# Moving a token block's second layer from float32r to float16 in a three-block attention and feed-forward kernel

## The chip, the cores and the metric

The kernel runs on one core of a Trainium2 chip. The metric is the time of the whole program on the device, in microseconds (us), as the median of several runs. A separate execution is recorded by the hardware profiler; everything said of engines comes from that one.

## The reference, cut to what matters

```
scores = scale * q @ k^T                      # 4 batches, 8 heads, 576 queries, 64 dims
thresh = max(scores) - tau                    # per query
scores = where(scores >= thresh, scores, -1e9)
x = softmax(scores) @ v                       # then heads side by side: x is 2304 x 512
xn = x / sqrt(mean(x*x) + 1e-6) * rms_g       # layer 1 only
y = (silu(xn @ w_gate) * (xn @ w_val)) @ w_out      # 512 -> 1536 -> 512
out = (silu(y @ w_gate2) * (y @ w_val2)) @ w_out2   # layer 2, without the norm
```

All inputs and outputs are float32.

## The kernel before, in words

The 2304 tokens are three blocks `b` of 768 (`TW`), each kept transposed as four chunks of 128 features. A block goes through attention, then the rms norm and layer 1 (`m` = 0), then layer 2 (`m` = 1). A layer is 18 units (`NU`): twelve gate/value units (`gate_val`) of 128 hidden features, with two out units (`outp`) behind every four of them; an out unit makes two of the four output chunks. Unit `n` counts through all blocks and layers, 36 per block: block 1's layer 1 is 36 to 53, its layer 2 is 54 to 71, block 2 has 72 to 89 and 90 to 107. The attention of block `b`+1 is laid between the units of block `b`; block 2's attention lies between units 36 and 53, in block 1's layer 1.

A float32 product is made of operands split into a high and a low part: high·high, high·low and low·high. An ordinary gate/value unit is 48 matmuls of 128 x 384 (`dense`, L1075). A seven-product unit (`gate_val7`, chosen by `fewer`) takes the fast 2 x 2 scheme with seven products of six matmuls (L1112), 42 in all. It needs four combinations of the input's quarters (`combine`: differences on VectorE L930, high parts on ScalarE L931, low parts L934) and, for each unit, sums of the weights' quarters (`weights7`: a load from the kept copy `kept`, four sums L1042, casts L1045, low parts L1047). Before, unit 54 is ordinary, 55 to 71 are seven-product units in float32r, and the gate/value units of 72 to 107 (`H16`) are seven-product units in float16.

Float16 needs scales, powers of two made from sums of squares. `square_sum` (L863, L864) loads a kept weight and squares it on ScalarE; `h_square` (L893) squares the hidden values of layer 1; `spread_sums` (L878) adds the partitions with a matmul; `power` (L869 to L872) makes the power of two in four VectorE steps; `unit_scales` (L887, L888) makes the factors of each unit. `y_scale` (L897 to L903) does this for layer 2's input and scales the layer-1 output `Y` on ScalarE; the last addition to `Y` (L1258) takes the same scale. The weights are scaled on ScalarE (L1040) ahead of their sums. Before, `square_sum` runs for block 2's layer-1 weights in block 1's layer 2, and for its layer-2 weights and out weights in block 2's layer 1.

`rms` makes the norm: the sums of squares of x (tile `SS`) by matmuls (L818), a reciprocal root in VectorE steps (L827 to L837), a spread over the partitions by matmuls (L849), and four multiplications (L858). `put` writes the high and low part of a layer's input (L952, L955). `split_h` makes high and low part of the hidden values (L1212, L1216).

What sets the order: every instruction is handed to `Program.op` with an engine, a cost, what it reads and writes, and a due time `p`, mostly the planned start of its unit `SU(n)` plus an offset of a table (`OFFS`, `GP`). `Program.order` runs a list scheduler over them, and each engine then does its instructions in that fixed order. All large transfers are issued by one queue, SP. While block 2's attention runs, gate and out products have two PSUM banks (`pt0`, `pt1`); four more (`pbPD`, `pbPA`, `pbPB`) come as the attention stages end.

## Time and profile before

| | us |
|---|---|
| median of 3 runs | 1145.5 (1144.47 to 1147.23) |
| profiled execution | 1140.48 |
| its span, first to last instruction | 1138.7 |
| units 36 to 53 (block 1, layer 1; attention of block 2) | 499 to 721 |
| units 54 to 71 (block 1, layer 2) | 721 to 868 |
| units 72 to 89 (block 2, layer 1) | 868 to 1003 |
| units 90 to 107 (block 2, layer 2) | 1003 to 1139 |

Busy time is the time in which an engine executes; for TensorE's matmuls, which overlap, the spacing from start to start is the price of one. The chain of waits goes back from the last instruction to what released it. A list of waits gives, for an engine, the line that waited, what ended the wait, and the total, the number and the longest in us.

### The profile page before, as it was taken

What the parts mean: (1) busy time and instruction counts of PE and PEld (TensorE: products, weight loads), DVE (VectorE), ACT (ScalarE), POOL (GpSimd) and SP (SyncE); (2) the same over time, 40 slices, a digit from 0 to 9 for tenths busy, and PEclk for the clock granted to TensorE, in tenths of its full rate; (3) what the DMA queues carried; (4) which work ended last, traced back from release to release, by engine and by line L of the source; (5) the groups of instructions that cost most, each with busy time, mean ns of one, the idle gap of its engine ahead of it and who ended that gap; (6) DMA issues with size and microseconds to landing.
All of it is one profiled execution on the core that took longest, in us unless ns stands there. A gap on an engine that the chain in (4) does not pass through costs nothing.

```text
span 1138.7 us, 19685 instructions
## 1 busy us (share of the span) xinstructions
PE 1106.7 (97%) x7106; PEld 965.3 (85%) x7106; DVE 906.8 (80%) x1631; ACT 791.4 (69%) x1175; POOL 630.6 (55%) x831
## 2 busy tenths in 40 slices
PE   8989999999999999999999999999999999999998
PEld 5656889989999989999999998999997768668677
DVE  7899498888987888887888887886688757985954
ACT  5798689878889887745866555756685766766631
POOL 5576145765668887449799875143413253234711
PEclk8999899999999999999999999999999999999999
DMA  6564349999999989958788786733755232122111
GB/s 186 172 221 143 103 126 288 266 268 305 236 243 261 237 266 262 262 177 198 165 188 184 182 187 147 260 110 128 255 191 178 74 115 98 60 108 93 37 39 56
DMA packets 178898, 201.44 MB, mean 177 GB/s; under 512 B 144368, under 2 KB 148208, under 8 KB 168816
## 3 DMA queue, kind: packets, MB, share of 16 engines
q1 hardware_dynamic: 178512, 200.18, 62.3%
q8 instruction: 56, 0.92, 0.3%
q14 instruction: 42, 0.34, 0.1%
q10 hardware_dynamic: 288, 0.00, 0.0%
HBM read 135.66 MB, written 36.18 MB: 151 GB/s over the span
## 4 chain that ended last, share of the span: by engine, by line
PE 60%; DVE 12%; DMA 10%; ACT 7%; POOL 6%; issue 4%; SPq 0%; ACTq 0%; POOLq 0%; DVEq 0%
PE ps L1075 20%; PE pbPA L1112 7%; PE pt L1112 7%; PE pbPB L1075 5%; DMA w<-kept 5%; PE pbPD L1075 5%; DMA arena<-arena 3%; PE pt L1075 3%; PE ps L719 2%; PE pt L772 2%; PE pt L675 2%; PE ps L615 2%; POOL arena L578 1%; PE pt L654 1%; ACT w L864 1%
## 5 line engine op out<-in xcount | busy, mean ns | idle before, releaser
L1075 PE MATMUL ps<-XS,w 128*128 128x384 f32 x1152 | 211.2, 340 | 2.6 <-DVE th L1194 1.4
L1075 PEld LDWEIGHTS ps<-XS,w 128*128 128x128 f32 x1152 | 200.6, 190 | 4.1 <-DVE th L1194 1.7
L1112 PEld LDWEIGHTS <-arena 128*128 128x128 f16 x1008 | 97.3, 98 | 65.7 <-issue 2.9
L1216 POOL TENSOR_TENSOR h<-th,h 128x384 fp32r<-128x384 f32 (+1 forms) x39 | 62.6, 1616 | 119.7 <-ACT h L1212 119.5
L1075 PE MATMUL pt<-XS,w 128*128 128x384 f32 x600 | 110.8, 337 | 2.8 <-DVE th L1178 2.8
L1075 PE MATMUL ps<-h,w 128*128 128x384 f32 x576 | 105.7, 338 | 2.6 <-DVE col L734 1.3
L1075 PEld LDWEIGHTS pt<-XS,w 128*128 128x128 f32 x600 | 103.0, 188 | 4.9 <-DVE th L1178 4.4
L1075 PEld LDWEIGHTS ps<-h,w 128*128 128x128 f32 x576 | 99.7, 188 | 4.9 <-issue 2.0
L735 ACT ACTIVATE arena<-ps,col 128x576 f32<-128x576 f32 x96 | 70.4, 736 | 39.4 <-DVE col L734 22.3
L733 DVE TENSOR_REDUCE col<-ps 128x1 f32<-128x576 f32 x96 | 71.4, 751 | 25.7 <-PE ps L719 25.6
L736 DVE SCALAR_TENSOR_TENSOR arena<-ps,col,arena 128x576 f32<-128x576 f32 x96 | 77.5, 810 | 14.5 <-ACT arena L735 13.9
L1075 PE MATMUL pbPB<-h,w 128*128 128x384 f32 x420 | 81.6, 340 | 1.9 <-DVE h L1216 1.8
L1212 ACT CAST h<-th 128x768 fp32r<-128x768 f32 x72 | 59.8, 832 | 33.9 <-DVE th L1175 13.2
L1112 PE MATMUL pt<-rx,arena 128*128 128x384 f16 (+1 forms) x384 | 82.9, 329 | 0.0
L1075 PE MATMUL pbPD<-h,w 128*128 128x384 f32 x420 | 79.9, 339 | 1.3 <-DVE h L1216 1.3
L578 POOL TENSOR_TENSOR arena<-arena 128x512 f16<-128x512 f32 x68 | 81.0, 1193 | 0.1
L1047 POOL TENSOR_TENSOR arena<-w,arena 128x384 f16<-128x384 f32 (+3 forms) x48 | 59.0, 1254 | 39.3 <-ACT arena L1045 39.1
L1112 PE MATMUL pbPA<-rx,arena 128*128 128x384 f16 (+1 forms) x368 | 78.7, 330 | 1.4 <-DVE X L858 0.9
L559 ACT ACTIVATE arena<-arena,col 128x576 f32<-128x576 f32 x76 | 65.0, 865 | 17.0 <-DVE col L746 9.3
L1075 PEld LDWEIGHTS pbPB<-h,w 128*128 128x128 f32 x420 | 73.4, 188 | 3.5 <-DVE h L1216 2.5
L1075 PEld LDWEIGHTS pbPD<-h,w 128*128 128x128 f32 x420 | 73.4, 188 | 2.2 <-DVE h L1216 1.7
L742 POOL TENSOR_SCALAR col<-col 128x1 f32<-128x1 f32 x96 | 32.7, 341 | 74.3 <-DVE arena L736 56.1
(274 smaller groups left out, 2733.5 us busy)
## 6 DMA issues: line engine op xcount, KB each, us to landing
w<-kept SPq DMA_DIRECT2D x77, 512.0 KB, 4.1
w<-in_w SPq DMA_DIRECT2D x36, 1024.0 KB, 7.0
w<-kept SPq DMA_DIRECT2D x25, 1024.0 KB, 5.7
kept<-w SPq DMA_DIRECT2D x17, 1024.0 KB, 5.3
kept<-w SPq DMA_DIRECT2D x26, 512.0 KB, 4.3
arena<-in_qkv SPq DMA_DIRECT2D x40, 160.0 KB, 4.3
ra<-in_qkv SPq DMA_DIRECT2D x10, 576.0 KB, 4.6
out<-Y SPq DMA_DIRECT2D x11, 384.0 KB, 2.7
```

Of the source, the lines that this page charges most:

```text
L559: op("ACT", 760, lambda: nc.scalar.activation(e, e, AF.Identity, bias=c[:, 4:5], scale=c[:, 3:4]), **k)
L578: op(en, 601 if eng == 2 else 1128, lambda: n1.tensor_tensor(h[:, 640:], e[:, :512], h[:, :512], ALU.subtract), lock=True, w=[("lo", n)], ...
L615: nc.tensor.matmul(s[m:m + w, jj, :b - a], x[k, c0:c0 + w], x[k, S + a:S + b], start=True, stop=True)
L733: op("DVE", 670, lambda: nc.vector.tensor_reduce(c[:, 0:1], s2, AX.XY, ALU.max, negate=True), w=[*sk, ("mx", n)], bufs=[cb], p=T + F['MAX' ...
L735: op("ACT", 640, lambda: nc.scalar.activation(e2, s2, AF.Exp, bias=c[:, 2:3], scale=SCALE), r=[("thr", n)], w=[*sk, ("e", n)] + ek, bufs=[ ...
L736: op("DVE", 750, lambda: nc.vector.scalar_tensor_tensor(e2, s2, c[:, 1:2], e2, ALU.is_ge, ALU.mult, accum_out=c[:, 6:7]), r=[("thr", n)], ...
L742: ns.tensor_scalar(cc(5), cc(6), 1e-9, 1.0 / UPP, ALU.add, ALU.mult)
L1047: op(en, 70 + (z - a) * 105 // 100 if en == "DVE" else 190 + (z - a) * 210 // 100, lambda a=a, z=z: n2.tensor_tensor(hv(1)[:, a:z], st[:, ...
L1075: nc.tensor.matmul(pt[:, j, :HT] if len(halves) == 2 else pt(), w(i, a), x(i, b_)[:, j * HT:(j + 1) * HT], start=(i == 0 and a == 0 and b_ ...
L1112: nc.tensor.matmul(bank(), w()[:, a, col * 256 + i * P:][:, :P], xf(i, b_), start=first and i == 0 and a == 0 and b_ == 0, stop=i == 1 and ...
L1212: op("ACT", 734, lambda: nc.scalar.copy(h[:, 0], tb.t), r=[("th", n)], w=[("h0", n)], bufs=[tb, hb], p=p + O(n)['HH'], name=f"h{n}")
L1216: op(eng, 72 + (z - a) * 105 // 100 if eng == "DVE" else 190 + (z - a) * 209 // 100, lambda a=a, z=z: n1.tensor_tensor(h[:, 1, a:z], tb.t[ ...
```

## The change

All gate/value units from 54 on are float16 seven-product units. `fewer` takes unit 54 in, `H16`, the float32r ring `r_s` and the code for it go, and `combine` and `put` write block 1's layer-2 input in float16.

The scales of layer 2 are made once, in block 1, and again only for block 2's own `Y`. The twelve layer-2 weight squares are ordered at units 32 to 37 (through the ring `w64`), the twelve layer-1 ones at units 45 to 57. `h_square` runs in block 1's layer 1 too, and reads the high part of `h`; a new `w_square` squares the six out weights as they are loaded for units 36 to 53. `weight_scales(1)` and `y_scale` come at the end of block 1's layer 1, with their sums in the bank `PD1`.

In block 1's layer 2 each unit's finished quarter weights, high and low part, 917 KB, are stored once in DRAM (`kept16`); in block 2's layer 2 a unit only loads them: no weight scaling, sums, casts or low parts there.

The tables are changed (a line or two stands in the diff), so that the block-2 attention ends about a unit earlier, and the order changes from about unit 26 on.

On TensorE the rms sums and the spread stood 13 rows apart before. In the rows, `h` are hidden values, `w` weights, `XS` the layer's input, `ps` the bank of the spread; rows with XS are unit 54.

```order
L818 MATMUL pbPD_5035<-small,SS 128x2 x6
L1075 MATMUL pt_74<-h_101,w_115 128x384 x3
...
L1075 MATMUL pt_75<-XS_94,w_113 128x384 x6
L1075 MATMUL pbPD_5034<-XS_94,w_113 128x384 x6
...
L1075 MATMUL pt_74<-XS_94,w_113 128x384 x6
L849 MATMUL ps_76<-ident,small 128x128 x6
L1112 MATMUL pt_75<-rx_1235,arena_7236 128x384
```

Now they stand in the out products of units 52 and 53, with the two scale sums (`sqt`, `hs`) between; the first row is the last PV product of the attention.

```order
L770 MATMUL pbPD_5080<-arena 64x256
L1073 MATMUL pt_75<-h_103,w_114 128x384 x3
...
L1073 MATMUL pt_74<-h_104,w_114 128x384 x3
L811 MATMUL pbPD_5080<-small,SS 128x2 x6
L872 MATMUL pbPD_5080<-sqt,small 128x12
L872 MATMUL pbPD_5080<-hs,small 128x2
L842 MATMUL ps_76<-ident,small 128x128 x6
L1073 MATMUL pt_75<-h_101,w_114 128x384 x3
```

The sums moved about a unit ahead, and the spread moved right behind them; the matmuls of unit 54 that stood between are now behind all out products.

On VectorE, before, the norm steps (L858) stood among the work of units 54 and 55.

```order
L1175 SCALAR_TENSOR_TENSOR th_105<-th_105,pt_74 128x384
L858 SCALAR_TENSOR_TENSOR X<-X,sqs,ps_76 128x768
L930 TENSOR_TENSOR Y<-Y 128x2x384
L858 SCALAR_TENSOR_TENSOR X<-X,sqs,ps_76 128x768
L1047 TENSOR_TENSOR arena_7236<-w_108,arena_7236 128x768
L1119 TENSOR_TENSOR tq<-tq,pbPD_5034 128x384
```

Now they stand, with weight sums (L1036) and weight low parts (L1041), between the last additions to `Y` (L1258), which free `pt0` and `pt1`.

```order
L866 TENSOR_SCALAR sqt<-sqt 128x1
L1036 TENSOR_TENSOR w_107<-w_107 128x256
...
L1036 TENSOR_TENSOR w_107<-w_107 128x256 x2
L1258 SCALAR_TENSOR_TENSOR Y<-pt_75,sqt,Y 128x384
L1258 SCALAR_TENSOR_TENSOR Y<-pt_74,sqt,Y 128x384
L851 SCALAR_TENSOR_TENSOR X<-X,sqs,ps_76 128x768
L1041 TENSOR_TENSOR arena_7240<-w_107,arena_7240 128x768
L851 SCALAR_TENSOR_TENSOR X<-X,sqs,ps_76 128x768
L1041 TENSOR_TENSOR arena_7240<-w_107,arena_7240 128x1024
L851 SCALAR_TENSOR_TENSOR X<-X,sqs,ps_76 128x768
L1258 SCALAR_TENSOR_TENSOR Y<-pt_75,sqt,Y 128x384
```

The norm steps moved from the seven-product work of the next layer into the out products of this one.

```
@@ -103,20 +103,20 @@
...
-UP, UP1, FP, T0, ATT, ATT2, LEAD, LEAD2, END2, UL, RMS0, RMS1, RMS2, CREL = 10682, 12700, 1362, 175757, 15789, 36712, 8.5, 11.0, 8.5, 25376, -397189, -61036, -1449640, 80130
+UP, UP1, FP, T0, ATT, ATT2, LEAD, LEAD2, END2, UL, RMS0, RMS1, RMS2, CREL = 10682, 11483, 1362, 175757, 15789, 74581, 8.5, 11.5, 13.5, 26563, -397189, -61036, -1840786, 80130
...
-GP = (-1.58, 2.78, 3.02, 4.13, 6.78, 2.5, 10.61, -1.35)
+GP = (-1.58, 3.02, 3.36, 5.34, 6.57, 3.92, 11.38, -1.31)
...
@@ -339,7 +339,6 @@
...
     rgx = SQS[:, 5, :4]
-    H16 = [SB0 + NU + i for i in GV]
@@ -399,13 +398,7 @@
...
     r_s16 = Ring([lambda k=k: again("arena", ARENA, 1)[:, k * 1792:(k + 1) * 1792].bitcast(F16).rearrange("p (a c) -> p a c", a=2) for k in range(6)])
-    xsb = Buf(None, None)
-    def old():
-        keys = [(f"XS{a}", c) for a in (0, 1) for c in range(NC)]
-        return list({pg.wrote[k] for k in keys} | {i for k in keys for i in pg.read.get(k, ())})
-    r_s = Ring([lambda i=i: again("arena", ARENA)[:, i * 3584:(i + 1) * 3584].rearrange("p (a c) -> p a c", a=2) for i in range(3)])
@@ -415,7 +408,7 @@
...
         tsb[0].ops = list(ops)
-        for b in r_s.slots:
+        for b in r_s16.slots:
@@ -859,9 +852,10 @@
...
     def square_sum(n, o, key, T):
-        b32 = r_w32.next()
-        op("DMA", 1500, lambda: nc.sync.dma_start(b32.t, kept2[n] if n in kept2 else f32(kept[n][:, 0])), r=[("kept", n)], w=[("sq32", n)], bufs=[b32], p=T - 6000, name=f"sq{n}")
-        op("ACT", 1100, lambda: nc.scalar.activation(b32.t.bitcast(BF16)[:, :1024], b32.t, AF.Square, accum_out=o), r=[("sq32", n)], w=[key], bufs=[b32], p=T + 6000, name=f"sq{n}")
+        b32 = r_w32.next() if n < NU else r_w64.next()
+        x = b32.t if n < NU else b32.t[:, :2048].bitcast(F32)
+        op("DMA", 1500, lambda: nc.sync.dma_start(x, kept2[n] if n in kept2 else f32(kept[n][:, 0])), r=[("kept", n)], w=[("sq32", n)], bufs=[b32], p=T - 6000, name=f"sq{n}")
+        op("ACT", 1100, lambda: nc.scalar.activation(x.bitcast(BF16)[:, :1024], x, AF.Square, accum_out=o), r=[("sq32", n)], w=[key], bufs=[b32], p=T + 6000, name=f"sq{n}")
@@ -874,12 +868,12 @@
...
 
-    def spread_sums(x, n, r, p):
-        op("PE", 300, lambda: nc.tensor.matmul(bank("PB1")[:, :n], ones[:, 0:1].to_broadcast([P, P]), x, start=True, stop=True), r=r, w=use("PB1"), p=p, name="scales", cols=0)
-    def weight_scales(m, p):
-        spread_sums(SETS16[m][0][:, :12], 12, [("SSQ", m)], p)
-        power(m, lambda: (bank("PB1")[:, :12], 1.0), ["PB1"], 0, 12, p)
+    def spread_sums(x, n, r, p, k="PB1"):
+        op("PE", 300, lambda: nc.tensor.matmul(bank(k)[:, :n], ones[:, 0:1].to_broadcast([P, P]), x, start=True, stop=True), r=r, w=use(k), p=p, name="scales", cols=0)
+    def weight_scales(m, p, k="PB1"):
+        spread_sums(SETS16[m][0][:, :12], 12, [("SSQ", m)], p, k)
+        power(m, lambda: (bank(k)[:, :12], 1.0), [k], 0, 12, p)
@@ -889,14 +883,20 @@
...
 
-    def h_square(f, n, tb, p):
-        op("ACT", 850, lambda: nc.scalar.activation(again("ra", 4 * S, 1).bitcast(BF16)[:, :TW], tb.t, AF.Square, accum_out=HQ[:, f:f + 1]), r=[("th", n)], w=["HSQ"], bufs=[tb], p=p, name=f"hsq{n}")
-    def y_scale(p):
-        for a, z, k in ((0, 12, "HSQ"), (12, 18, "HSW")):
-            op("DVE", 75, lambda a=a, z=z: nc.vector.tensor_reduce(HQ[:, 18 + a // 12:19 + a // 12], HQ[:, a:z], AX.X, ALU.add), r=[k], w=["HB"], p=p, name="scales")
-        spread_sums(HQ[:, 18:20], 2, ["HB"], p)
-        op("DVE", 75, lambda: nc.vector.tensor_scalar(HQ[:, 20:22], bank("PB1")[:, :2], 1.0, 0.0, ALU.mult, ALU.add), w=["PB1", "HB"], p=p, name="scales")
+    def h_square(f, n, hb, p):
+        jb = r_t.next() if n < SB0 else None
+        junk = (lambda: jb.t.bitcast(BF16)[:, 1024:1024 + TW]) if jb else (lambda: again("ra", 4 * S, 1).bitcast(BF16)[:, :TW])
+        op("ACT", 850, lambda: nc.scalar.activation(junk(), f32(hb.t[:, 0]), AF.Square, accum_out=HQ[:, f:f + 1]), r=[("h0", n)], w=["HSQ"], bufs=[hb] + [jb] * (n < SB0), p=p, name=f"hsq{n}")
+    def w_square(n, sbf, i, p):
+        junk = r_t.next()
+        op("ACT", 1100, lambda: nc.scalar.activation(junk.t.bitcast(BF16)[:, 1024:], f32(sbf.t[:, 0]), AF.Square, accum_out=HQ[:, 12 + i:13 + i]), r=[("wh", n)], w=["HSW"], bufs=[sbf, junk], p=p, name=f"wsq{n}")
+    def y_scale(p, k):
+        for a, z, r in ((0, 12, "HSQ"), (12, 18, "HSW")):
+            op("DVE", 75, lambda a=a, z=z: nc.vector.tensor_reduce(HQ[:, 18 + a // 12:19 + a // 12], HQ[:, a:z], AX.X, ALU.add), r=[r], w=["HB"], p=p, name="scales")
+        spread_sums(HQ[:, 18:20], 2, ["HB"], p, k)
+        op("DVE", 75, lambda: nc.vector.tensor_scalar(HQ[:, 20:22], bank(k)[:, :2], 1.0, 0.0, ALU.mult, ALU.add), w=[k, "HB"], p=p, name="scales")
@@ -917,7 +917,7 @@
...
 
-        gen = int(cb == NB - 1)
+        gen = 1
@@ -947,8 +947,6 @@
...
         hi, lo = [lambda a=a: XSF(gen)[:, a, c] for a in (0, 1)]
-        if gen == 1:
-            bufs = bufs + [Buf(None, xsb)]
@@ -962,7 +960,7 @@
...
     def fewer(n):
-        return n > SB0 and n % (2 * NU) in GV
+        return n >= SB0 and n % (2 * NU) in GV
@@ -987,6 +985,8 @@
...
             op("DMA", 3000, lambda: nc.sync.dma_start(f32(ws), kept[i]), r=[("kept", i)], w=[("wh", n), ("wl", n)], bufs=[sbf], p=T - 20000, name=f"load_{n}")
+            if 36 <= n < SB0 and i not in GV:
+                w_square(n, sbf, [4, 5, 10, 11, 16, 17].index(i), T - 5000)
@@ -1018,34 +1018,32 @@
...
 
+        sbf = wsp[n] = r_s16.next()
+        hv = lambda a: sbf.t()[:, a]
+        if n >= SB0 + 2 * NU:
+            op("DMA", 2800, lambda: nc.sync.dma_start(sbf.t(), kept16[i]), r=[("kept16", i)], w=[(k, n, x) for k in ("wh", "wl") for x in (True, False)], bufs=[sbf], p=T + O(n)['WL'], name=f"load_{n}")
+            return
         stb = r_w64.next()
-        if n not in H16:
-            sbf = wsp[n] = r_s.next()
...
 
-        h16 = n in H16
-        if h16:
-            if n == H16[0]:
-                xsb.ops = old()
-                for x in r_s16.slots:
-                    x.ops = [o for y in r_s.slots + tsb for o in y.ops]
-            sbf = wsp[n] = r_s16.next()
-        hv = lambda a: sbf.t()[:, a]
         p = T + O(n)['WS2']
-        if h16:
-            j, k = divmod(H16.index(n), NF)
-            op("ACT", 939, lambda c=SETS16[j][2][:, k:k + 1]: nc.scalar.activation(st[:, :1024], st[:, :1024], AF.Copy, scale=c), r=[("SC", j, 0)], w=[("w32", n)], bufs=[stb], p=p, name=f"w_scale{n}")
+        j, k = divmod(GV.index(i), NF)
+        op("ACT", 939, lambda c=SETS16[j][2][:, k:k + 1]: nc.scalar.activation(st[:, :1024], st[:, :1024], AF.Copy, scale=c), r=[("SC", j, 0)], w=[("w32", n)], bufs=[stb], p=p, name=f"w_scale{n}")
...
             for a, z in [(a, z)] if en == "DVE" else [(a, (a + z) // 2), ((a + z) // 2, z)]:
-                op(en, 70 + (z - a) * 105 // 100 if en == "DVE" else 190 + (z - a) * 210 // 100, lambda a=a, z=z: n2.tensor_tensor(hv(1)[:, a:z], st[:, a:z], (hv(0) if h16 else f32(hv(0)))[:, a:z], ALU.subtract), lock=True,
+                op(en, 70 + (z - a) * 105 // 100 if en == "DVE" else 190 + (z - a) * 210 // 100, lambda a=a, z=z: n2.tensor_tensor(hv(1)[:, a:z], st[:, a:z], hv(0)[:, a:z], ALU.subtract), lock=True,
                    r=[("w32", n), ("wh", n, late)], w=[("wl", n, late)], bufs=[stb, sbf], p=p + 1000, name=f"w_split{n}")
+        if n < SB0 + NU:
+            op("DMA", 2800, lambda: nc.sync.dma_start(kept16[i], sbf.t()), r=[(k, n, x) for k in ("wh", "wl") for x in (True, False)], w=[("kept16", i)], bufs=[sbf], p=T - 2000, name=f"keep16_{n}")
+    kept16 = {i: dr.tile([P, 2, 1792], F16, name=f"kept16_{i}") for i in GV[NF:]}
@@ -1091,14 +1089,14 @@
...
                 wb = wsp[n]
-                (b1, k1), (b2, k2), (b3, k3) = SETS[(f if b > 1 else f + 1) % 2]
+                (b1, k1), (b2, k2), (b3, k3) = SETS[(f + (b == 1 and f > 0)) % 2]
...
                 t2 = tb.t.rearrange("p (j s) -> p j s", j=2)
-                h16 = n in H16
-                gen = int(b == NB - 1)
+                h16 = True
+                gen = 1
@@ -1146,7 +1144,7 @@
...
                 if h16 and m == 0:
-                    h_square(f, n, tb, p + O(n)['HH'])
+                    h_square(f, n, hh[f], p + O(n)['HH'])
@@ -1177,6 +1175,8 @@
...
                     split_h(f, n, tb, T + 2 * U + O(n)['DR'])
+                    if m == 0:
+                        h_square(f, n, hh[f], T + 2 * U + O(n)['DR'] + O(n)['HH'])
@@ -1255,10 +1255,10 @@
...
                             else:
-                                op("DVE", 480, lambda y=y, x=x, neg=m == 1 and q == 2, last=-1.0 if m == 1 and q == 2 else SETS16[1][2][:, 12:13] if b == NB - 1 and q == 2 else 1.0: nc.vector.scalar_tensor_tensor(y, x(), last, y, ALU.mult, ALU.subtract if neg else ALU.add), r=[("SC", 1, 12)] if b == NB - 1 and q == 2 and m == 0 else [], w=[key, ("Y", o)], p=Tj + Uj + O(n)['DR'] + O(n)['YY'], name=f"y{n}")
+                                op("DVE", 480, lambda y=y, x=x, neg=m == 1 and q == 2, last=-1.0 if m == 1 and q == 2 else SETS16[1][2][:, 12:13] if q == 2 else 1.0: nc.vector.scalar_tensor_tensor(y, x(), last, y, ALU.mult, ALU.subtract if neg else ALU.add), r=[("SC", 1, 12)] if q == 2 and m == 0 else [], w=[key, ("Y", o)], p=Tj + Uj + O(n)['DR'] + O(n)['YY'], name=f"y{n}")
...
                             if m == 0:
-                                put(o, Y[:, o], [("Y", o)], [], T + U + O(n)['DR'] + O(n)['PUT'], ("POOL", "DVE")[8 * b + 4 + o in P_E], HT if o < 2 and b > 1 else TW, int(b > 1))
+                                put(o, Y[:, o], [("Y", o)], [], T + U + O(n)['DR'] + O(n)['PUT'], ("POOL", "DVE")[8 * b + 4 + o in P_E], HT if o < 2 and b else TW, int(b > 0))
@@ -1293,16 +1293,12 @@
...
                         unit_scales(0, T)
-                if b == NB - 1 and m == 0:
-                    for i in (2 * f, 2 * f + 1):
-                        if i < NF:
-                            square_sum(GV[NF + i], SETS16[1][0][:, i:i + 1], ("SSQ", 1), T)
-                        elif i < 18:
-                            square_sum(OUTS[i - 12], HQ[:, i:i + 1], "HSW", T)
-                    if f == 6:
-                        weight_scales(1, T)
+                if b == 1 and m == 0:
+                    square_sum(GV[NF + f], SETS16[1][0][:, f:f + 1], ("SSQ", 1), T)
                     if f == NF - 1:
-                        y_scale(SU(base + GV[f] + 1))
+                        weight_scales(1, T, "PD1")
+                if b and m == 0 and f == NF - 1:
+                    y_scale(SU(base + GV[f] + 1), "PD1" if b == 1 else "PB1")
```

## Rows read from the trace of the kernel before

**Rows 1.** The page: busy time of each engine, and the granted clock in slices.
```profile
PE 1106.7 (97%) x7106; PEld 965.3 (85%) x7106; DVE 906.8 (80%) x1631; ACT 791.4 (69%) x1175; POOL 630.6 (55%) x831
...
PEclk8999899999999999999999999999999999999999
```

**Rows 2.** Windows: stretch, us, PE, PEld, DVE, ACT, POOL busy, clock, DMA share, GB/s.
```profile
499.00:685.00 186.00, 183.36 (x1235) 172.98 (x1234) 157.15 (x352) 117.56 (x200) 153.88 (x240) 1.00 0.77 180
685.00:745.00 60.00, 56.63 (x349) 52.04 (x348) 46.69 (x88) 39.80 (x64) 16.90 (x20) 1.00 0.74 211
745.00:868.00 123.00, 120.61 (x684) 118.88 (x685) 93.06 (x140) 78.30 (x126) 46.72 (x37) 1.00 0.48 168
868.00:1003.00 135.00, 133.72 (x800) 99.68 (x798) 100.25 (x171) 94.32 (x144) 51.14 (x51) 1.00 0.30 105
1003.00:1138.70 135.70, 132.33 (x794) 98.68 (x792) 89.34 (x131) 64.32 (x96) 47.59 (x41) 1.00 0.16 59
```

**Rows 3.** Chain of waits: start, us, what; float32r at 761, float16 at 892.
```profile
760.96 3.15 PE pbPA L1112 x18
...
892.08 2.92 PE pbPA L1112 x18
```

**Rows 4.** The page's groups: weight loads in float16 and float32r; busy, mean ns.
```profile
L1075 PEld LDWEIGHTS ps<-XS,w 128*128 128x128 f32 x1152 | 200.6, 190 | 4.1 <-DVE th L1194 1.7
L1112 PEld LDWEIGHTS <-arena 128*128 128x128 f16 x1008 | 97.3, 98 | 65.7 <-issue 2.9
```

**Rows 5.** PE's waits, 685 to 745 us: total, times, longest.
```profile
PE pt L1075 <- DVE th L1175: 1.5, 1, 1.5
PE pbPA L1112 <- DVE X L858: 0.9, 1, 0.9
PE pt L1075 <- DVE th L1178: 0.7, 1, 0.7
```

**Rows 6.** PE's waits, 745 to 1139 us, all of them.
```profile
PE pbPB L1075 <- DVE h L1216: 1.8, 1, 1.8
PE pbPD L1075 <- DVE h L1216: 1.3, 1, 1.3
PE pbPA L1112 <- ACT SS L1121: 0.5, 1, 0.5
```

**Rows 7.** Timeline of PE, start and us: rms sums and their spread.
```profile
717.85 1.39 PE L818 MATMUL pbPD<-small,SS 128*128 128x2 f32 x12
...
729.87 1.60 PE L849 MATMUL ps<-ident,small 128*128 128x128 f32 x12
```

**Rows 8.** Timeline of DVE: first and last step of the earlier root chain.
```profile
487.09 0.16 DVE L827 TENSOR_SCALAR small<-pt 128x6 f32<-128x6 f32 x1
...
490.06 0.15 DVE L837 SCALAR_TENSOR_TENSOR small<-small 128x6 f32<-128x6 f32 x1
```

**Rows 9.** DVE operations: groups (ns min/median/max) of L1042 and L1047; timeline rows.
```profile
L1042 DVE TENSOR_TENSOR w<-w x100: 404/418/2078, 474.1 to 1080.5; 128x256 f32<-128x256 f32 x100
...
L1047 DVE TENSOR_TENSOR arena<-w,arena x46: 947/1212/2169, 721.4 to 1085.1; 128x768 f16<-128x768 f32 x15, 128x1024 f16<-128x1024 f32 x15, 128x768 fp32r<-128x768 f32 x8, 128x1024 fp32r<-128x1024 f32 x8
...
732.31 1.00 DVE L858 SCALAR_TENSOR_TENSOR X<-X,sqs,ps 128x768 f32<-128x768 f32 x1
...
994.00 0.62 DVE L1258 SCALAR_TENSOR_TENSOR Y<-pbPB,sqt,Y 128x384 f32<-128x384 f32 x1
```

**Rows 10.** ACT operations: groups of the squares, and the timeline row of Y's scaling.
```profile
L864 ACT ACTIVATE w<-w x30: 1050/1058/1072, 653.6 to 841.9; 128x1024 bf16<-128x1024 f32 x30
L864 ACT ACTIVATION_READ_ACCUMULATOR w<-w x30: 185/187/204, 654.6 to 842.9; 128x1 f32 x30
...
L893 ACT ACTIVATE ra<-th x12: 829/840/858, 881.6 to 987.6; 128x768 bf16<-128x768 f32 x12
...
992.49 3.42 ACT L903 ACTIVATE Y<-Y,sqt 128x768 f32<-128x768 f32 x4 [0.20 <-DVE sqt L871]
```

**Rows 11.** DMA issues of kept weights: KB each, us from issue to landing.
```profile
w<-kept SPq DMA_DIRECT2D x77, 512.0 KB, 4.1
```

20 lines of the change are left out of this document (10 added, 10 removed), and 6 rows, old and new, of the table OFFS.

## The prediction

> **What bounds the kernel now.** First the page's shares: TensorE (PE) is busy for 97% of the span, VectorE (DVE) for 80% [rows 1]. Then the windows by stage [rows 2]: after the first 499 us PE idles 2.6 us of 186, 3.4 of 60, 2.4 of 123, 1.3 of 135 and 3.4 of 136. So the time is the number of matmuls times their spacing, and what can be won or lost is the spacing and those few idle microseconds. The granted clock is 1.00 in all these stages, the upper level of 2.4 GHz. Third the chain of waits, which gives the spacing: 18 seven-product matmuls of 384 columns take 3.15 us in float32r and 2.92 us in float16, 175 and 162 ns each [rows 3]. The columns are the same; what differs is the weight load in front, 190 ns against 98 [rows 4]. Last the waits of PE in the second block's passage from its first to its second layer (685 to 745 us) and in what follows [rows 5, 6]; these are the waits that the change touches.
>
> The profiled execution took 1140.48 us (span 1138.7), the median of the three timed runs is 1145.5. I make the sum of differences against the profiled span and apply it to the median: nothing in the sum depends on the 5 us between them.
>
> **A, the matmuls.** Eleven units of 42 seven-product matmuls and one ordinary unit of 48, 510 at 175 ns in float32r, become twelve units of 42, 504 at 162 ns in float16: 89.2 - 81.8 = 7.4 us; with the spacing rounded the other way (174 and 163 ns) 6.6. I take **-7.0 us**. The whole stretch from 745 to 868 us is PE-bound (120.6 of 123 us busy), so this comes through as long as VectorE, 93 us there [rows 2], keeps up, and it gives up nothing but gains nothing: the float32r casts and low parts become float16 ones of the same size.
>
> The Trainium skill (TensorE: Matmul & The Clock Gate, Back-to-back issue gap) states about 131 ns for 512 columns as the sustained spacing of load and matmul pairs, with N/2.4 + 2.5 ns as the isolated one. My estimate from its figures for 384 columns is 98 ns sustained, by which A would be about -40 us; the rows in float16 stand at 162 ns, the isolated figure, so the measurement decides.
>
> **B, the passage of block 1 from layer 1 to layer 2.** Here lies what the change costs. Before, the rms sums (L818) and the spread of the result (L849) stood 12 us apart on PE, with ordinary matmuls of unit 54 between [rows 7], and the spread waited for nothing. Now the rms sums, both scale sums and the spread stand directly behind one another, between out units. Term by term, in PE waits:
> - The sums wait for the squares of block 2's last attention tile. Behind the last PV product stand 18 matmuls, 3.2 us, where before there were 30, 5.3 us. What PV's evacuation, squares and additions need beyond 3.2 us I estimate at 1.4 us.
> - The spread waits for the reciprocal root, twelve dependent steps, each 0.2 us from start to start in the earlier copy of that chain (487.09 to 490.06 us for 12 steps and one long operation between) [rows 8]: 2.1 us. The scale chain lies in between its steps, as it did there, so it adds little.
> - The next out product needs a bank whose evacuation (L1258, now with the new scale) stands on VectorE behind four weight sums, 4 x 0.42 us [rows 9], and behind the scaled Y on ScalarE, four in 3.42 us [rows 10]: 1.6 us after what the spread's matmuls cover.
> - The product after the next waits for L1258 behind three norm steps of 1.00 us and two low parts of 0.95 and 1.21 us [rows 9], 5.2 us. They begin when the second of two evacuations ends, 0.5 us after the first; with the next evacuation's own 0.6 us that is 6.3 us from the first one's end, of which two products of 2.1 us cover 4.2: 2.1 us.
> - Unit 54 is now a seven-product unit and needs combinations of x (difference, cast, low part) and weights with their sums one unit earlier than before, behind the same VectorE rows: up to 4 us.
>
> Together up to 11.5 us, less the 3.4 us that PE idles in this stretch now [rows 2, 5]: +8.1. At the other end only the root chain and the two bank waits stay: 5.8 - 3.4 = +2.4. I take **+4.6**, nearer the low end, because the 1.5 us that PE waits there now for VectorE's work on the last hidden features [rows 5] gets attention matmuls in front of it in the new order, and because each wait in the row gives VectorE time that shortens the next.
>
> The Y scaling itself is hidden if the bank wait above is its whole effect; uncovered it would cost its 3.42 us, which is within the upper end.
>
> **C, the waits between 745 and 1139 us.** PE waits 1.8 us for the low part of h at 855 us, 1.3 at 990 and 0.5 for a ScalarE evacuation [rows 6]. The 30 squares of 1.06 us with their reads of 0.19 us that ScalarE did from 653.6 to 841.9 us [rows 10] are gone from here, so the third goes; of the other two I expect half. **-2.0** (between -3.6 and -0.5). In block 2's layer 2 the weight scaling, sums, casts and low parts are gone, but no PE wait after 1003 us is listed [rows 6], so that is worth nothing; the stored pieces come in as 12 loads of 917 KB in place of 512 KB over a DMA that is 16% busy there [rows 2, 11], a load now landing in 4.1 us against units of some 7 us: nothing either. The twelve stores go out between 745 and 868 us at a share of 0.48, on SP's queue, where a store that waits for its low part holds up the next loads; units there are loaded two ahead, so nothing, or up to 1 us.
>
> **D, units 32 to 53.** The attention of block 2 must now be done about one unit (10.3 us) earlier, and ScalarE gets 18 squares more in this window (12 of h, 6 of w) at 0.84 and 1.06 us, each with a read of 0.19 [rows 10], 20 us on top of 118 of 186: it has room. Pool is busy 154 and VectorE 157 of 186 us [rows 2]; in 176 us that is 87 and 89%. So it fits, with little slack. PE idles 2.6 us there, so the bounds are -1 and about half a unit, +5; I take **+0.9**, the twelve early weight squares at units 32 to 37 included, whose loads meet a DMA that is 81% busy on the mean of that stage.
>
> **Sum:** -7.0 + 4.6 - 2.0 + 0.9 = -3.5 us; 1145.5 - 3.5 = **1142.0 us**.
>
> **The rivals.**
> - *The passage eats the gain.* B at its upper end, everything else as above: -7.0 + 8.1 - 2.0 + 0.9 = 0.0, 1145.5 us. For it: a list of waits each behind a named row. Against it: waits in a row partly absorb one another, since a late PE gives VectorE time. Within C's and D's bounds it runs from 1143.2 to 1147.8.
> - *Attention ends late* (slower). Its last products and the rms sums stand one unit earlier in PE's fixed order; if VectorE and Pool, 157 and 154 us of work, do not get it done in 176 us, PE stands at the rms sums and everything behind them. At three quarters of a unit, 8 us in place of D's 0.9, the sum is +3.6: 1149.1 us. It decides from 6.7 us of lateness, where the sum passes +2.3. For it: 89% busy on VectorE, and two PSUM banks alone for gate tiles. Against it: all of this stage cost PE only 2.6 us at 84% and 83%.
> - *The waits overlap.* B at its low end and C in full: -7.4 + 2.4 - 3.6 + 0.9 = -7.7, 1137.8 us. For it: now 12 us lie between sums and spread and nothing waits; against it: the twelve steps are now bare.
> - *The clock falls.* The granted clock stays 1.00 over waits of 1.8 us [rows 2, 6]; it is lower in two of the first five slices of the span, the first of them the start, where PE begins [rows 1]. If the waits in B join to several microseconds and the clock halves to 1.2 GHz for the next 24 matmuls, these cost 24 x 0.162 = 3.9 us more: 1145.9 us. By the Trainium skill (the same page, Part 1: The HAM clock gate) an idle array falls back to 1.2 GHz and needs activity to come back; no trace here shows it in this stretch.
> - That the change doesn't do what it says can be left out: the order of instructions has the 504 float16 matmuls and no weight preparation in block 2's second layer.
>
> **How the numbers follow.** What a measurement can tell from no change is 0.2%, 2.3 us. Chances: the forecast (1138.5 to 1143.2) 0.38; overlapping waits 0.11; the passage eats the gain 0.24; the clock 0.05; attention late, or the passage beyond its end, 0.22. The forecast and the overlap are faster: 0.49, of which I leave 0.01 to the edge. Same: 0.24 + 0.05 + 0.01 = 0.30. Slower: 0.22. The range from 1136.5 (A at -7.4, B at +2.4, C at -3.6, D a little under nothing) to 1149.0 (attention late by most of a unit) leaves out some 2 in 10.
>
> **What would show it.** The spacing in the chain between 745 and 868 us should be 162 ns and that stretch about 7 us shorter (A). PE's waits in the passage should name the spread (L842), the sums (L811) and the out products on L1258, with 6 to 11 us together against 3.4 (B). The waits for h at the two later passages should be smaller, and after the last passage PE should idle as now, while VectorE's busy time falls (C). Units 36 to 51 should take as long as before (D): if they take longer, attention was late, and the prediction is wrong on that side; if the spread waits for nothing it is wrong on the other.

## The result

The changed kernel takes 1152.2 us (1151.3 to 1153.9) against 1145.0 for the kernel before: a ratio of 1.0061 with a 95% interval of 1.0044 to 1.0079. It is slower by 7 us where 3.5 us less were forecast, and outside the stated range. The profiled execution took 1151.4 us, its span 1149.3; the profile of before lies 4.5 us under its median, so differences of the two profiles (10.6 us) come out 3 to 4 us too large in sum.

The page of the changed kernel, lines as in [rows 1]:

```profile
PE 1105.3 (96%) x7102; PEld 928.4 (81%) x7102; DVE 863.1 (75%) x1576; ACT 786.9 (68%) x1182; POOL 617.3 (54%) x827
...
PEclk9999999999999999999999999899999999999999
```

TensorE is busy for about as long as before and VectorE for 44 us less, but the span is longer: the span less TensorE's busy time is 44.0 us, 32.0 before. The windows say where TensorE idles, with the columns of [rows 2]. They lie at the same times as those of before, though the changed kernel is up to 18 us behind.

```profile
499.00:685.00 186.00, 176.62 (x1179) 164.96 (x1178) 156.81 (x345) 136.63 (x240) 146.90 (x226) 0.99 0.88 208
685.00:745.00 60.00, 52.70 (x322) 47.00 (x321) 45.40 (x104) 39.92 (x66) 19.32 (x28) 0.94 0.67 189
745.00:868.00 123.00, 119.15 (x711) 86.10 (x710) 89.61 (x140) 77.45 (x113) 49.10 (x44) 1.00 0.50 174
868.00:1003.00 135.00, 133.44 (x798) 99.49 (x798) 87.41 (x138) 84.31 (x131) 67.78 (x65) 1.00 0.39 131
```

TensorE now idles 9.4 us of the 186 (2.6 before) and 7.3 of the 60 (3.4 before), and the granted clock is 0.94 in the second. After that it idles 3.9 us of 123 and 1.6 of 135, not far from the 2.4 and 1.3 of before. TensorE's waits from 499 to 685 us:

```profile
PE ps L712 <- DVE arena L729: 3.3, 3, 1.2
PE ps L712 <- ACT ps L1359: 2.5, 1, 2.5
PE pt L1073 <- DVE Y L1258: 1.6, 1, 1.6
PE pt L1073 <- DVE th L1176: 1.3, 1, 1.3
```

Scores (L712) wait for the softmax of an earlier tile (L729), once for a constant that ScalarE writes (L1359), and gate and out products (L1073) for evacuations. From 685 to 745 us it is the passage to layer 2:

```profile
PE pt L1073 <- DVE Y L1258: 3.8, 3, 3.0
PE ps L842 <- DVE small L830: 1.1, 1, 1.1
```

On TensorE's timeline (start, us, [idle before <- what ended it]) it looks so:

```profile
717.14 0.39 PE L872 MATMUL pbPD<-sqt,small 128*128 128x12 f32 x2 [0.26 <-DVE small L820]
717.84 0.38 PE L872 MATMUL pbPD<-hs,small 128*128 128x2 f32 x2 [0.30 <-DVE sqt L863]
719.36 1.94 PE L842 MATMUL ps<-ident,small 128*128 128x128 f32 x12 [1.14 <-DVE small L830]
724.25 5.82 PE L1073 MATMUL pt<-h,w 128*128 128x384 f32 x24 [2.96 <-DVE Y L1258]
```

The longest wait, 2.96 us, can be followed back through ScalarE and VectorE:

```profile
719.26 1.06 ACT L858 ACTIVATE w<-w 128x1024 bf16<-128x1024 f32 x1 [2.68 <-DMA w<-kept]
...
721.48 0.43 DVE L1036 TENSOR_TENSOR w<-w 128x256 f32<-128x256 f32 x1 [2.09 <-ACT w L1034]
```

ScalarE stands 2.68 us at the square of a layer-1 weight whose load is late; in its fixed order the weight scaling of unit 54 (L1034) comes after it, VectorE's weight sums wait for that, and the evacuation that frees the bank (L1258) stands behind the sums. Then the 24 matmuls take 5.82 us where 4.2 would do: their starts stand 0.32 us apart up to 727.3 us and 0.173 from then on, because the granted clock had fallen. Read in windows of 1 us, it is 0.50 (1.2 GHz) from 721 to 727 us and 1.00 (2.4 GHz) from 728. It had fallen at 720.5 us, ahead of the longest wait.

```profile
720.00:725.00 5.00, 2.04 (x11) 1.75 (x10) 3.48 (x9) 5.00 (x8) 2.38 (x3) 0.55 0.33 123
725.00:730.00 5.00, 5.00 (x23) 4.75 (x22) 4.92 (x6) 5.00 (x7) 1.67 (x2) 0.77 0.01 6
```

It was also at the lower level from 502.0 to 505.4 us, right behind the wait of 2.5 us for the constant, where scores start 0.24 us apart in place of 0.13:

```profile
495.00:505.00 10.00, 7.45 (x39) 7.22 (x38) 6.92 (x9) 7.99 (x14) 5.46 (x6) 0.85 0.99 327
```

In the kernel before it is 1.00 from 400 us to the last unit.

What was won stands in the chain of waits, in float16 where before it was float32r: the spacing of [rows 3], 162 ns, now from 745 us on. Unit 54 begins at 739.7 us (721.3 before; units counted by their matmuls) and unit 72 at 878.5 (868.4): layer 2 of block 1 gives back 8.3 us of the 18.4 lost by then. Both figures contain the spread, some 1.5 us, which stood in unit 54 before [rows 7] and now stands ahead of it.

```profile
806.83 2.92 PE pbPA L1110 x18
```

### The profile page after: what moved, and what is told of

Its sections match the earlier page's. It is cut to its first block, busy times and chain, and to the rows that moved or that the text cites. A ratio compares the mean times of both kernels' runs of the same rounds, so it can differ in the third digit from the quotient of the medians.

```text
span 1149.3 us, 19617 instructions
## 1 busy us (share of the span) xinstructions
PE 1105.3 (96%) x7102; PEld 928.4 (81%) x7102; DVE 863.1 (75%) x1576; ACT 786.9 (68%) x1182; POOL 617.3 (54%) x827
## 4 chain that ended last, share of the span: by engine, by line
PE 65%; DVE 14%; ACT 8%; DMA 8%; issue 4%; SPq 0%; POOL 0%; ACTq 0%; DVEq 0%
PE ps L1073 15%; PE pt L1110 9%; PE pbPA L1110 8%; PE pt L1073 6%; PE pbPB L1073 6%; PE pbPD L1073 5%; DMA w<-kept 5%; PE ps L712 3%; PE pt L668 2%; PE pt L765 2%; PE ps L608 2%; PE pt L647 1%; PE pbPB L1110 1%; PE pbPD L1110 1%; DVE col L726 1%
## 5 line engine op out<-in xcount | busy, mean ns | idle before, releaser
L1110 PEld LDWEIGHTS <-arena 128*128 128x128 f16 x1512 | 145.7, 98 | 105.2 <-issue 10.9
L1073 PE MATMUL ps<-XS,w 128*128 128x384 f32 x1152 | 210.6, 339 | 3.0 <-DVE th L1194 1.4
L1073 PEld LDWEIGHTS ps<-XS,w 128*128 128x128 f32 x1152 | 199.5, 189 | 5.2 <-DVE th L1194 1.7
L1216 POOL TENSOR_TENSOR h<-th,h 128x384 fp32r<-128x384 f32 (+1 forms) x46 | 67.7, 1482 | 122.0 <-ACT h L1212 121.8
L1073 PE MATMUL pt<-XS,w 128*128 128x384 f32 x576 | 106.7, 339 | 2.5 <-DVE th L1176 2.2
L1073 PE MATMUL ps<-h,w 128*128 128x384 f32 x576 | 105.7, 338 | 1.5 <-DVE Y L1276 0.6
L1073 PEld LDWEIGHTS pt<-XS,w 128*128 128x128 f32 x576 | 99.4, 189 | 5.0 <-DVE th L1176 3.6
L1073 PEld LDWEIGHTS ps<-h,w 128*128 128x128 f32 x576 | 99.9, 188 | 3.4 <-DVE Y L1276 1.0
L1110 PE MATMUL pt<-rx,arena 128*128 128x384 f16 x456 | 86.5, 326 | 3.5 <-ACT tq L1119 2.8
L729 DVE SCALAR_TENSOR_TENSOR arena<-ps,col,arena 128x576 f32<-128x576 f32 x96 | 77.4, 811 | 12.4 <-ACT arena L728 11.5
L1073 PE MATMUL pbPB<-h,w 128*128 128x384 f32 x420 | 82.8, 342 | 0.5 <-DVE h L1216 0.4
L1073 PE MATMUL pbPD<-h,w 128*128 128x384 f32 x420 | 80.2, 340 | 0.4 <-DVE h L1216 0.4
L712 PE MATMUL ps<-rx 128*128 128x288 f32 x416 | 72.6, 303 | 8.2 <-DVE arena L729 5.5
L735 POOL TENSOR_SCALAR col<-col 128x1 f32<-128x1 f32 x96 | 35.1, 365 | 78.9 <-DVE arena L729 61.5
L1110 PE MATMUL pbPA<-rx,arena 128*128 128x384 f16 x408 | 77.4, 326 | 0.0
L1073 PEld LDWEIGHTS pbPB<-h,w 128*128 128x128 f32 x420 | 73.6, 188 | 2.3 <-DVE h L1216 1.1
L1073 PEld LDWEIGHTS pbPD<-h,w 128*128 128x128 f32 x420 | 73.6, 188 | 1.4 <-DVE h L1216 0.8
L712 PEld LDWEIGHTS ps<-rx 128*128 128x128 f32 x416 | 63.0, 190 | 14.2 <-DVE arena L729 8.8
```

Of the source, the lines that this page charges most:

```text
L712: nc.tensor.matmul(s[:, j, :HS], x[:, c:c + P], x[:, k:k + HS], start=i + u == 0, stop=i == 1 and u == len(heads) - 1)
L729: op("DVE", 750, lambda: nc.vector.scalar_tensor_tensor(e2, s2, c[:, 1:2], e2, ALU.is_ge, ALU.mult, accum_out=c[:, 6:7]), r=[("thr", n)], ...
L735: ns.tensor_scalar(cc(5), cc(6), 1e-9, 1.0 / UPP, ALU.add, ALU.mult)
L1073: nc.tensor.matmul(pt[:, j, :HT] if len(halves) == 2 else pt(), w(i, a), x(i, b_)[:, j * HT:(j + 1) * HT], start=(i == 0 and a == 0 and b_ ...
L1110: nc.tensor.matmul(bank(), w()[:, a, col * 256 + i * P:][:, :P], xf(i, b_), start=first and i == 0 and a == 0 and b_ == 0, stop=i == 1 and ...
L1216: op(eng, 72 + (z - a) * 105 // 100 if eng == "DVE" else 190 + (z - a) * 209 // 100, lambda a=a, z=z: n1.tensor_tensor(h[:, 1, a:z], tb.t[ ...
```

## The experiments

Ratios are to the kernel before as it ran beside each kernel (its medians are 1142.4 to 1143.6 us), with 95% intervals; the changed kernel stands at 1.0061. Idle time is a window less TensorE's busy time in it.

### Single suspects

Suspects that the profile names were moved, shrunk or filled one at a time, without another change of the order. `put_after(a, b)` moves one instruction behind another in the list that the scheduler hands out.

```
+    put_after(at("ACT", "sq7"), at("ACT", "y_scale", 3))
+    put_after(at("DMA", "sq9"), at("ACT", "sq7"))
```

> The changed kernel with one square of a layer-1 weight (and the load that takes its buffer next) moved behind the four scalings of Y in the passage of block 1 from layer 1 to layer 2; nothing else moves. Theory 1 (ScalarE stands at that square for a load of 2.7 us, and weight scaling, weight sums, the evacuation and TensorE stand behind it): TensorE's wait of 3.0 us for the evacuation shrinks to under 1 us, the clock keeps 1.00 there, 1147 to 1149 us in place of 1152.2. Rival, theory 2 (the chain of root and scale steps and the norm steps on VectorE set the passage): the wait stays, 1151.5 to 1152.5.

1.0066 (1.0042 to 1.0089). The wait at the first bank goes, and comes back one product later:

```profile
726.52 4.46 PE L1073 MATMUL pt<-h,w 128*128 128x384 f32 x24
732.92 10.27 PE L1073 MATMUL pt<-h,w 128*128 128x384 f32 x48 [1.95 <-DVE Y L1258]
```

The late load was the last of several things that are late at the same place: counted from the rms sums (L811), unit 54 begins 1.0 us earlier than in the changed kernel, and unit 56 begins 1.3 us later than there. The 48 matmuls behind the wait take 10.3 us in place of 8.4, so the clock still falls.

```
+    put_after(at("ACT", "sq25"), at("ACT", "K1", 3))
```

> The changed kernel with one early square of a layer-2 weight moved behind ScalarE's copy of the constant into the bank of the first scores of block 2's attention; nothing else moves. Theory 1 (a late load of a square holds that copy and TensorE for 2.5 us, and the clock falls to 0.85 there): 1148.5 to 1150 us in place of 1152.2. Rival (the attention of block 2 is bound by VectorE and Pool, so that what is won at 502 us is lost again by 620): 1152.

1.0062 (1.0039 to 1.0085): nothing. Unit 36 begins 3.4 us earlier than in the changed kernel (500.8 against 504.2), and the clock does not fall there; unit 45 begins only 0.2 us earlier (611.5 against 611.7).

```
-        op("ACT", 850, lambda: nc.scalar.activation(junk(), f32(hb.t[:, 0]), AF.Square, ...
+        op("ACT", 850, lambda: nc.scalar.activation(*((junk()[:, :1], f32(hb.t[:, 0])[:, :1]) if n < SB0 else ...), AF.Square, scale=27.712 if n < SB0 else 1.0, ...
...
+        op("ACT", 1100, lambda: nc.scalar.activation(junk.t.bitcast(BF16)[:, 1024:1025], f32(sbf.t[:, 0])[:, :1], AF.Square, scale=32.0, ...
```

> The changed kernel with the 18 squares of block 1's layer 1 (12 of h, 6 of out weights) taken over one column in place of 768 and 1024, scaled up; same order. It leaves out most of the sums of squares. Theory 3 (these 20 us of ScalarE work make the softmax of block 2 late, TensorE waits 5 to 6 us for it between 610 and 664 us): 1147 to 1149 us. Rival (the attention is late because it is due one unit earlier, whatever ScalarE does): 1151 to 1152.

1.0064 (1.0039 to 1.0090): nothing, with 10 us less on ScalarE between 435 and 660 us. Then the norm's spread and steps were put back where the kernel before had them:

```
+    put_after(at("PE", "rms_spread2"), at("PE", "mm54", 3))
+    put_after(at("DVE", "norm0", -1), at("DVE", "ev54", 0))    # norm1 to norm3 likewise, behind ev54 1, ev54 2 and gv54 0
```

> The changed kernel with the spread of the norm moved on TensorE from between the out products into unit 54, behind four of its seven products, and the four norm steps moved on VectorE among unit 54's evacuations, as the kernel before had it; the rest in the same order. Theory 2 (the bare chain and the norm steps between the evacuations make the passage's waits): the waits for the root (1.4 us) and for the evacuations behind the norm steps go, 1147.5 to 1149.5 in place of 1150.6. Theory 1 (the late load): 1150 to 1151.

1.0092 (1.0068 to 1.0116), no gain: the bank's evacuation is what is late, and TensorE waits for it 5.9 us in one piece in place of several. The clock falls here too: the 72 matmuls take 15.4 us where 12.6 would do.

```profile
723.85 15.42 PE L1073 MATMUL pt<-h,w 128*128 128x384 f32 x72 [5.88 <-DVE Y L1258]
```

And the idle time was filled:

```
+            for t in range(16 if b == NB - 1 else 0):
+                nc.tensor.matmul(bank("PD1")[:, :HT], XSF()[:, 0, 0][:, :P], XSF()[:, 0, 1][:, :HT], start=True, stop=True)
```

> The changed kernel with 16 matmuls of 384 columns more, right behind the spread of the norm, which write a bank that nobody reads then. They fill 2.6 us of the idle time before the next out product. If the clock's fall is a cost of its own (the 24 matmuls behind the wait take 5.8 us in place of 4.2): the clock keeps 1.00 there, and the time falls by 1.5 to 2.5 us against the changed kernel, though more is computed. If the clock only falls because nothing is waiting for it: no change, or up to 2.6 us slower.

1.0082 (1.0059 to 1.0106). The out products behind run at full speed again, 24 in 4.35 us, but the spread and the filler pay: 16 in 3.7 us, 0.23 each. The clock fell at 723.1 us, ahead of the filler, and was back at 726.5; in the changed kernel it was low from 720.5 to 727.3. The filler shortened the fall, did not prevent it, and cost its own time.

```profile
722.50 2.44 PE L842 MATMUL ps<-ident,small 128*128 128x128 f32 x12 [1.14 <-DVE small L830]
724.60 3.89 PE L844 MATMUL pbPD<-XS 128*128 128x384 f32 x16
728.32 4.35 PE L1075 MATMUL pt<-h,w 128*128 128x384 f32 x24
```

Last, the making of scales in block 1 was filtered out of the list, and constants set to 1.

```
+    L = [i for i in L if i not in gone]     # gone: layer-2 squares, scale sums and steps, y_scale of block 1
```

> The changed kernel without the making of scales in block 1: no squares of layer-2 weights, of h and of out weights there, no scale sums, no scaling of Y; the scales are 1. The rest in the same order. It tells what float16 gives without its preparation. If the preparation is all of the loss: 1145 - 7 - 2 = 1136 us. If the squeezed attention and the passage's norm steps are what costs: 1146 to 1149.

1.0043 (1.0029 to 1.0057): 2 us better with intervals that overlap, and still slower than before. The filter goes by name and leaves four of the twelve squares of h in (units 36 to 39, 4 us of ScalarE); float16, unit 54 and the stored weights stay as well. TensorE idles 8.2 us from 435 to 660 us, 9.5 in the changed kernel, 2.7 before. So none of theories 1 to 3 explains the loss: what costs there is hardly an instruction that is new.

### Order and work apart

Code and tables were crossed, and the changed code was given old tables without scales:

```
 x: changed code,            NORM_E ... XO_E of the kernel before
 y: code of the kernel before, NORM_E ... XO_E of the changed kernel
 z: as x, and
-                if b == 1 and m == 0:
+                if False:                  # likewise no h_square, w_square, y_scale in block 1
```

> The changed kernel's code with the tables of numbers of the kernel before (due times, offsets, engine choices); the scheduler makes its own order from them. If the new due times of block 2's attention cost the 6 to 8 us of waits between units 30 and 51: 1143 to 1146 us. If the new work itself (squares, scales, float16 unit 54) costs it: 1150 or more, since the tables were not made for this work.

> The kernel before with the changed kernel's tables; no float16 in block 1, no new squares. If the tables' earlier attention costs 6 to 8 us by itself: 1150 to 1152. If it does not: 1143 to 1146, as before.

> The changed kernel's code with the tables of the kernel before and without the scales of block 1 (no squares of layer-2 weights, h or out weights there, no scale sums, no scaling of Y; the scales are 1): float16 and seven products from unit 54 on, and the stored weights, alone. If float16 gives what its spacing says and the loss is the preparation and the new due times: 1134 to 1139 us, below the kernel before. If any change of the order in units 27 to 54 costs as much as the changed kernel's: 1143 to 1150.

1.0235 (1.0207 to 1.0262), 1.0293 (1.0265 to 1.0320) and 1.0163 (1.0139 to 1.0187). Each is slower than both parents. From 435 to 660 us TensorE idles 8.9, 10.5 and 9.6 us: the same loss with the new work or without it, with the old tables or the new. In the first the attention also ends late, and the rms sums wait for it, which they do not in the changed kernel:

```profile
PE pbPD L811 <- DVE X L799: 7.1, 1, 7.1
```

The second loses most in block 1's layer 2, units 54 to 71, which take 164 us in place of 147; the cause of that is open. The common loss led to theory 4: the order of the kernel before fits these stages, and any other order costs about this. The kernel before was shaken:

```
+        d = _rng.uniform(-500, 500)            # second run: 1500
+        if 400000 < pg.prio[i] < 720000:
+            pg.prio[i] += d
```

> The kernel before with every due time between 400 and 720 us shifted at random by up to 0.5 us; same work, nearly the same order. Theory 4 (the order of the attention stage was fitted to the chip, and every other order of the same work costs several us of TensorE waits there): 1147 to 1155 us. If the loss of the changed kernel is due to its new work or its earlier attention: 1143 to 1146.

> The same with shifts of up to 1.5 us, other random numbers. Theory 4: 1148 to 1160 us, more than with 0.5 us. Otherwise 1143 to 1147.

1.0106 (1.0081 to 1.0132) and 1.0323 (1.0296 to 1.0349). With not one instruction changed, TensorE's waits from 435 to 660 us become

```profile
PE ps L719 <- DVE arena L736: 2.9, 3, 1.8
PE ps L719 <- POOL rx L537: 2.7, 1, 2.7
PE ps L719 <- POOL rx L535: 2.6, 1, 2.6
```

That is 9.9 us of idle time, the changed kernel's size, where the order as given has 2.7. In the windows of the kernel before, the changed one and the shaken one, in this order:

```profile
435.00:660.00 225.00, 222.33 (x1450) 209.53 (x1449) 190.51 (x393) 146.15 (x227) 174.00 (x253) 1.00 0.82 201
435.00:660.00 225.00, 215.50 (x1396) 201.76 (x1395) 184.13 (x381) 165.73 (x270) 166.44 (x238) 0.99 0.89 223
435.00:660.00 225.00, 215.06 (x1374) 201.16 (x1373) 183.04 (x375) 139.34 (x217) 168.17 (x241) 0.98 0.78 194
```

The waits are only half of what the shake costs. Over the whole span TensorE idles 7 us longer than before, and it is busy 8 us longer with the same 7106 matmuls. The granted clock is at its lower level from 510.2, 558.0 and 639.9 us on, for some 3 us each time, behind the waits of 2.6, 2.7 and 1.8 us, and twice more after 860 us. One random draw was run for each size of shake, so how far draws differ is not shown.

### Orders fitted with equal effort

So the work can only be priced in orders that fit. From 395 us on, the scheduler's list was improved by moving one instruction at a time within its dependencies, keeping what shortens the sequence by the kernel's own costs and latencies. Engines, buffers and instructions stay. Of one to five such rows of trials for a kernel the best was run, of the changed kernel the best two; so the effort is alike, not exactly equal.

```
-    for i in pg.order():
+    for i in FITTED:
         pg.fn[i]()
```

> The kernel before in an order improved in the same way, by the same number of steps. It tells what the comparison of two orders made with equal effort gives. Theory 4 with nothing left to gain in the kernel before (its order was fitted already): 1141 to 1145. If equal effort helps both alike: 1133 to 1138, below both kernels.

> The changed kernel, the same instructions on the same engines and the same buffers, in an order that was improved by moving one instruction at a time (from 395 us on) as long as the waits that follow from the kernel's own costs and latencies shrink. Theory 4 (the loss lies in the order, not in the work): 1139 to 1145 us, in place of 1150 to 1152, with TensorE's waits between 435 and 660 us down from 11 to under 5. If the new work needs its time in any order: 1148 to 1152.

> The changed kernel in a second order improved in the same way from the same start with other random numbers. It shows how far two fitted orders of one kernel lie apart: within 3 us of the first if the fit finds what the work allows, more if it is luck.

> The changed kernel without the making of scales in block 1 (no squares of layer-2 weights, h and out weights there, no scale sums, no scaling of Y; the scales are 1), in an order improved in the same way. If float16 is worth its spacing once the order fits: 6 to 8 us below the kernel before in its improved order, and 8 to 14 us below the changed kernel in its own, which then is the price of the scales. If float16 gives nothing even so: the same as the kernel before, improved.

> The changed kernel with its 30 squares for layer 2 made, but the scale sums, the power-of-two steps and the scaling of Y in block 1 left out (scales are 1), in an order improved like the others. It splits the 10 to 14 us between the fitted kernel without scales (1126) and the fitted changed kernel (1136 to 1140). If the passage's chain (scale sums, steps, scaled Y before the banks come free) is the price: 1126 to 1130. If the squares' work and loads on ScalarE and the load queue are: 1134 to 1138.

> The changed kernel without stored quarter weights (block 2's second layer scales, sums, casts and splits them again), in an order improved like the others. With the scheduler's order it took 1172. If the stores and loads are worth nothing, as predicted: 1136 to 1141, like the changed kernel fitted. If the preparation costs TensorE time in block 2's second layer: 1142 or more.

| in a fitted order | us (range) | ratio (95%) | TensorE idle 435 to 660, 660 to 770 |
|---|---|---|---|
| kernel before | 1131.8 (1130.6 to 1133.9) | 0.9904 (0.9878 to 0.9930) | 2.7, 1.1 |
| float16, no scales | 1126.3 (1126.1 to 1127.1) | 0.9856 (0.9832 to 0.9881) | 2.5, 3.1 |
| the same with the squares | 1133.6 (1131.4 to 1135.4) | 0.9914 (0.9897 to 0.9931) | 3.1, 7.9 |
| changed kernel, first fit | 1140.5 (1138.4 to 1142.9) | 0.9976 (0.9959 to 0.9993) | 6.1, 6.2 |
| changed kernel, second fit | 1136.2 (1135.4 to 1137.4) | 0.9941 (0.9921 to 0.9962) | 4.1, 4.9 |
| changed kernel, weights not stored | 1144.8 (1142.8 to 1148.4) | 1.0018 (1.0003 to 1.0032) | 7.1, 6.4 |

By the ratios the changed kernel gains 10 to 14 us from order alone, and is then 2 to 6 us faster than the kernel before as it was given. The kernel before gains 11 us in the same way, so it was not at its end either, and its fitted order is the fastest complete kernel here, 1131.8 us, faster than both. Its gain does not lie where the changed kernel lost: from 435 to 660 us it idles 2.7 us in both orders, and 4 us are gained by unit 54 and 5 in block 1's layer 2. A fitted order of float16 without scales idles 2.5 us there, so not every other order costs what theory 4 says.

With like effort the change costs 4.4 to 8.7 us, about the 7 us that it costs as given: order moves both kernels, and the difference that is left is the work's, as far as one fit of the kernel before can tell. What order decides is where the time goes. From 435 to 660 us the changed kernel idles 6.8 us more than the kernel before as given, and 1.4 and 3.4 us more in the fits; from 660 to 770 us it is 8.5 as given and 3.8 and 5.1 in the fits, where the clock falls too (it does not in the fitted kernel before).

Float16, unit 54 and the stored weights bring 5.5 us (1131.8 to 1126.3). The squares then cost 7.3 (6.6 by the ratios, since the two did not run side by side), with TensorE idling 7.9 us in place of 3.1 from 660 to 770 us, and the chain of sums, steps and scaled Y another 2.6 to 7.0. Two fits of one kernel lie 4.3 us apart. The 5.5 and the lower 4.4 stand hardly above that, and smaller differences between rows are not told by one fit each, the chain's share among them. In the second fit of the changed kernel these TensorE waits from 435 to 660 us are left:

```profile
PE ps L774 <- DVE arena L791: 1.2, 1, 1.2
PE pt L1135 <- DVE th L1235: 1.2, 2, 0.6
PE pt L1135 <- DVE Y L1320: 0.9, 1, 0.9
PE ps L774 <- POOL XS L1015: 0.5, 1, 0.5
```

Weights not stored, in the scheduler's own order:

```
-        if n >= SB0 + 2 * NU:
+        if False:                   # no load of kept16; the store likewise
```

> The changed kernel without the stored quarter weights: block 2's second layer scales, sums, casts and splits them again, as before; no stores. If the stores on the load queue hold up units 55 to 60: 1147 to 1149 us. If the prediction's 'worth nothing' holds on both sides: 1150 to 1153, like the changed kernel.

1.0262 (1.0234 to 1.0291), 1172 us: much worse, but the tables were made for stored weights. Fitted, 1144.8 is 4.3 to 8.6 us above the changed kernel's two fits, at the edge of what two fits differ by; that storing helps is likely and its size is open.

## Why the prediction was wrong

**A was right.** -7.0 us were forecast. Layer 2 of block 1 takes 8.3 us less, with the 162 ns that were read ahead. 1.5 us of that is the spread, which moved ahead of it, and TensorE idles 1.1 us more in this layer (4.7 against 3.6, with 4.3 at units 54 and 55), so the matmuls themselves give some 7.9.

**D failed.** It was put at +0.9 us with bounds of -1 and +5; TensorE's idle time from 499 to 685 us rose by 6.8. The step that failed is "So it fits, with little slack": it took a stage's room from its engines' busy shares (84 to 89%) and its price from the 2.6 us of waits that it had. Those waits belonged to one order. The shaken kernel has the same work, VectorE no busier (81% from 435 to 660 us, 85% before), and 9.9 us of idle time; the changed kernel with the same work in fitted orders idles 4.1 and 6.1 us there in place of 9.5. So most of D is order, and 1.4 to 3.4 us remain for the work. Units 36 to 51 take 204 us in place of 196, the sign that the prediction had named for this side; some 3 us of that is attention that now stands earlier. The rival "attention ends late" was looked for at the rms sums; they waited in the crossed kernel with old tables and do not wait here, while waits of 1 to 2.5 us are spread over the stage.

**B was sized too low.** +4.6 us were forecast with +8.1 as its upper end. From 685 to 770 us TensorE idles 10.6 us, 3.4 before: +7.3, within the bounds, but not by the terms as they were sized. The sums waited for nothing in place of 1.4 us, the spread 1.1 for the root in place of 2.1, the scale sums 0.6 where nothing was counted. The first evacuation took 3.0 in place of 1.6, since the load of a square held ScalarE in front of it, the later ones 0.9 in place of 2.1, and units 54 and 55 waited 4.3 where up to 4 was allowed. (The terms as listed add up to 11.2 us, not 11.5, so the upper end should have been +7.8.) Loads of squares were weighed under D alone, for the early ones; that a layer-1 square stood ahead of the weight scaling on ScalarE was not seen. "Each wait in the row gives VectorE time that shortens the next" was wrong for the longest: VectorE waited too, 2.09 us.

**The clock rival came true, and in two places.** In the passage 24 matmuls take 5.8 us in place of 4.2 and the spread 1.9 in place of 1.5, some 2 us; the fall at 502 us costs some 1.5 us more, in a stage for which no fall was named. Together it is near the 3.9 us that were priced with a chance of 0.05.

**C came out right in size, in part by luck.** Apart from units 54 and 55, TensorE's listed waits from 745 us on fell from 3.6 us to 1.9, near the -2.0 forecast. But the waits for h, of which half were to go, fell from 3.1 to 0.8, and the wait for a ScalarE evacuation, which was to go, is 1.1 in place of 0.5. Unit 90 begins 9.8 us late and unit 107 10.3, so the preparation that went from there gave nothing, as said; under a fitted order that is no longer sure.

Of the 18.4 us by which unit 54 begins late, 6.8 are D, 4.3 the part of B that lies ahead of it, some 3.5 the clock, and 2.4 the spread, which came behind its start before, with the new scale sums; 1.4 us are not accounted for. 8.3 come back in layer 2. That leaves 10 us in the profiles and 7 in the medians.

## What to carry to other kernels

A change that makes a scheduler lay a stage out anew can lose several us there whatever the change is worth, here 6.8 us in one stage of 186; a shake of due times by half a microsecond, with no change at all, cost 12 us of 1142. Such a shake is one run, though one draw does not tell the size closely. Low waits in the profile of before belong to its order, not to the load of its engines, and are no bound for a stage that is laid out anew. Compare the work of two versions in orders fitted with like effort, and fit one of them twice to see how far luck goes: here order moved both kernels by 10 us or more, and the difference between them hardly changed.
